# Another order of the front and some order ties in a three-layer kernel (attention, gated MLP, mixture of experts)

## The chip, the cores and the metric

The kernel runs on one core of a Trainium2 chip. The metric is the device time of one execution in microseconds. A core has a matrix engine (TensorE, PE in the profile), a vector engine (VectorE, DVE), an activation engine (ScalarE, ACT), a general engine (GpSimd, POOL), and a queue that issues the transfers (SyncE, SP). They run beside each other and wait for one another by semaphores; each works through its own instructions in the order in which the program put them.

## The reference, cut to what matters

Three layers follow one another. B=4 batches, 8 heads, S=576 positions, head size 64, 32 memory slots; 2304 tokens of width 512.

```python
a   = softmax(phi, over the sequence)            # 4 x 8 x 576 x 32 features, weights over slots
k_m = einsum('bhsm,bhsd->bhmd', a, k);  v_m = einsum('bhsm,bhsd->bhmd', a, v)
att = softmax(q @ k_m^T / 8);           x = att @ v_m         # -> 2304 x 512
x   = (sigmoid(x @ w_gate) * (x @ w_val)) @ w_out             # gated MLP, inner width 1536
p   = x @ w_gate2 + log1p(exp(x @ w_noise)) * noise           # router, top 2 of 8 experts
out = sum over the two experts: weight * relu(x @ w1[e]) @ w2[e]
```

## The kernel before

**What is computed where.** Nearly every product is made in fp16, with each fp32 operand split into a high and a low half, so that a product costs three matmuls. `memory` (L181) turns the features of one batch and one half of the heads (a "group", g=0 or 1): five transposes of phi against the identity `idf` (L189, L194), 40 small matmuls against the keys and values (L204), and a scaled copy `km` (L206). `attention` (L268) makes the scores of the queries (L284, L281) in three blocks: two large half blocks (u=0, 1: 512 columns) and a small one (u=2). For each block DVE takes the maximum `smx` (L288) and subtracts it (L292), ACT takes the exponential (L293). `normalised` (L296) sums and takes the reciprocal on DVE and multiplies on POOL (L304), and `turned` (L307) transposes the result on PE (L312) into the high and low halves of `x` (L321 on ACT, L322 on DVE).

**Stage 1** (L473) multiplies x with weights in which v_m is already contained: `fold(b, u)` (L245) scales v_m (POOL `vs`, L252), multiplies it with the weights of unit u (PE `pv`, L259, 32 records), and splits the product into `wq`: high half by ACT (L261), low half by DVE (L263; for the very first unit L1090). A unit and chunk of stage 1 are 24 matmuls (L485), a tanh on ACT (L487), a gate on DVE (L489), and a split into `gT` on ACT (L490) and DVE (L491). **Stage 2** multiplies gT with w_out (L502); `tokens` (L504) then takes the largest absolute value `am` of a tile on DVE (L514), scales it, and stores it for the experts.

**Weights.** w_gate, w_val and w_out come as halves of 512 KB. `rounded` (L368) turns one half in four steps: ACT L372, DVE L376 and L377, POOL L378. Two halves make one tile `w_n` (or `wo_n` for w_out), whose square sum (ACT L401, or L418 for w_out, into `wom`) goes through a matmul with ones (PE L93) and some short steps on DVE (L101 to L106) and POOL (L449, L450); only then is the scale known that `fold` needs. At the end the six w_out tiles are split by L434 (`split`: ACT, then DVE, 1024 columns). A buffer of a half is loaded again when it has been turned.

**What sets the order.** The program is written as generators. `turns` (in `build`) advances the attention generator and the weights generator; a list scheduler then orders each engine's instructions by priority, and `behind(d, o)` ties instruction d behind o on the same engine without a semaphore. At the start `turns(atts, atts, atts)` and FIRST=5 steps of `weights` come first; `half` then alternates a half of the weights with a step of the attention until the first x is there. `att_first_loads` (L168) gives the order of the first transfers on SP. Later `beside` runs the other batches, the folds, the tokens, and `presplits` (L680), which splits experts' weights ahead.

## Time and profile before

| | |
|---|---|
| runs of the kernel before | 852.46, 852.05, 851.23 us; median 852.05 us |
| profiled execution | 851.26 us, of which span 849.4 us, 1.86 us around it |
| mean granted TensorE clock | 0.991 |
| PE busy | 799.7 us of the span (94%) |
| DVE, ACT, POOL busy | 454.8, 440.0, 233.5 us |

Times in the profile count from the span's start. In the list by slices PE is 9 tenths busy or more from slice 5 on nearly everywhere; the first two slices (42 us) are the thin ones. So the table of all engines says that PE is the bound, and only the stretches where it waits can be shortened: the front up to the start of stage 1 (the first L485), and single waits after it.

### The profile page before, as it was taken

The numbers are of one execution on the slowest core, as the hardware profiler recorded it, in microseconds if no ns is written. First come the engines' busy times: TensorE is split into PE (matmuls) and PEld (weight loads), VectorE is DVE, ScalarE is ACT, GpSimd is POOL, SyncE is SP. The second block draws the span as 40 slices with busy tenths as digits, with TensorE's granted clock in tenths as the row PEclk, the third lists the DMA queues.
The fourth block names the chain that finished last, engine by engine and source line by source line (L and its number), as shares of the span: only waits on it lengthen the run. The fifth ranks groups of instructions, "written<-read, shape, count | busy, mean of one in ns | idle before, by whom it ended". The sixth has DMA issues, their size and how long they took to land.

```text
span 849.4 us, 16715 instructions
## 1 busy us (share of the span) xinstructions
PE 799.7 (94%) x6531; PEld 526.3 (62%) x6531; DVE 454.8 (54%) x1221; ACT 440.0 (52%) x859; POOL 233.5 (27%) x257
## 2 busy tenths in 40 slices
PE   5699889999999998999999999999999999999995
PEld 3478756476677665776556555746657475574752
DVE  3798996464558687645472365544445343450210
ACT  4687795155354665534263576645457364461320
POOL 1755650102203030231135342023133231232012
PEclk9999899999999999999999999999999999999998
DMA  9987669230312655617938899536767757463113
GB/s 315 349 263 242 231 202 319 78 106 2 76 58 98 181 172 151 215 47 184 280 103 217 167 240 208 176 75 129 190 150 126 207 117 171 74 124 39 23 23 40
DMA packets 124609, 130.95 MB, mean 154 GB/s; under 512 B 71664, under 2 KB 88176, under 8 KB 124144
## 3 DMA queue, kind: packets, MB, share of 16 engines
q1 hardware_dynamic: 114480, 109.10, 44.6%
q0 software_dynamic: 10048, 20.76, 13.5%
q8 instruction: 52, 0.85, 0.4%
q14 instruction: 29, 0.24, 0.1%
HBM read 85.87 MB, written 28.76 MB: 135 GB/s over the span
## 4 chain that ended last, share of the span: by engine, by line
PE 77%; DVE 9%; ACT 6%; DMA 3%; issue 2%; POOL 1%; SPq 0%; another core or an unknown queue 0%; DVEq 0%; ACTq 0%; POOLq 0%
PE ph L852 24%; PE py L866 23%; PE px L502 14%; PE pg L485 10%; PE pa L284 2%; PE pv L259 1%; DMA w<-wg 1%; DVE wq L263 1%; DVE pw L376 1%; DVE gT L491 1%; DVE pg L489 1%; PE pa L204 1%; ACT gT L490 1%; DMA wsp<-hl 1%; PE pl L530 1%
## 5 line engine op out<-in xcount | busy, mean ns | idle before, releaser
L485 PE MATMUL pg<-x,wq 128*128 128x192 f16 x1728 | 162.8, 249 | 11.7 <-DVE gT L491 4.2
L866 PEld LDWEIGHTS <-hT 128*128 128x128 f16 (+1 forms) x960 | 99.8, 105 | 104.8 <-DVE hT L858 1.2
L485 PEld LDWEIGHTS <-wq 128*128 128x128 f16 x1728 | 145.4, 99 | 31.2 <-issue 18.5
L502 PE MATMUL px<-wo,gT 128*128 128x512 f16 x648 | 147.7, 379 | 0.0
L874 POOL DMA_INDIRECT out<-y,mts x40 | 65.3, 1633 | 206.7 <-ACT y L873 204.3
L866 PE MATMUL py<-w2a,hT 128*128 128x512 f16 (+1 forms) x480 | 105.3, 379 | 0.7 <-DVE hT L858 0.7
L866 PE MATMUL py<-w2b,hT 128*128 128x512 f16 (+1 forms) x480 | 104.9, 379 | 0.0
L502 PEld LDWEIGHTS <-gT 128*128 128x128 f16 x648 | 61.7, 98 | 67.9 <-issue 2.3
L852 PE MATMUL ph<-xe,w1a 128*128 128x312 f16 (+2 forms) x768 | 103.3, 296 | 0.0
L852 PE MATMUL ph<-xe,w1b 128*128 128x312 f16 (+2 forms) x768 | 103.0, 296 | 0.0
L858 DVE TENSOR_TENSOR hT<-r,hT 128x312 f16<-128x312 f32 (+2 forms) x128 | 57.4, 480 | 84.7 <-ACT hT L857 78.6
L873 ACT ACTIVATE y<-py,css 128x512 f32<-128x512 f32 (+1 forms) x40 | 27.5, 687 | 124.5 <-PE py L866 115.5
L852 PEld LDWEIGHTS <-w1b 128*128 128x128 f16 x768 | 75.2, 98 | 27.1
L852 PEld LDWEIGHTS <-w1a 128*128 128x128 f16 x768 | 75.0, 98 | 27.1
L856 ACT ACTIVATE r<-ph 128x312 f32<-128x312 f32 (+2 forms) x128 | 49.7, 429 | 74.8 <-PE ph L852 68.6
L656 POOL DMA_INDIRECT meta<-mt,vi x36 | 38.5, 1069 | 121.3 <-DVE vi L653 81.1
L837 POOL DMA_INDIRECT xg<-xs,mts x40 | 45.2, 1130 | 81.5 <-DMA xe<-xg 47.7
L490 ACT ACTIVATE gT<-pg 128x384 f16<-128x384 f32 x72 | 35.1, 487 | 52.6 <-DVE pg L489 46.3
L487 ACT ACTIVATE sg<-pg,gss 128x384 f32<-128x384 f32 x72 | 41.9, 582 | 34.5 <-PE pg L485 33.6
L489 DVE SCALAR_TENSOR_TENSOR pg<-sg,pg 128x384 f32<-128x384 f32 x72 | 40.2, 558 | 35.0 <-PE pg L485 17.3
L857 ACT CAST hT<-r 128x312 f16<-128x312 f32 (+2 forms) x128 | 53.2, 458 | 0.9
L871 DVE TENSOR_TENSOR css<-mts,iw 128x1 f32<-128x1 f32 (+1 forms) x40 | 6.4, 163 | 87.3 <-ACT y L873 80.7
(241 smaller groups left out, 951.1 us busy)
## 6 DMA issues: line engine op xcount, KB each, us to landing
wo<-w SPq DMA_DIRECT2D x52, 512.0 KB
st<-kv SPq DMA_DIRECT2D x16, 512.0 KB
w<-wo SPq DMA_DIRECT2D x12, 512.0 KB
f<-w SPq DMA_DIRECT2D x12, 512.0 KB
wsp<-hl SPq DMA_DIRECT2D x12, 512.0 KB
out<-z SPq DMA_DIRECT2D x23, 256.0 KB
xs<-row SPq DMA_DIRECT2D x18, 256.0 KB
st<-q SPq DMA_DIRECT2D x6, 576.0 KB
```

The source lines that it names most:

```text
L485: self.gated = nc.tensor.matmul(p[:, f, :], w[:, l, g, j, f * P : (f + 1) * P], x[:, r, g, ch * QC : (ch + 1) * QC], start=n == 0, stop=n ...
L487: self.tanh = nc.scalar.activation(sg, ps[0], AF.Tanh, scale=self.gs[(b, u)])
L489: nc.vector.scalar_tensor_tensor(pv, sg, 1.0, pv, op0=ALU.add, op1=ALU.mult)
L490: self.gate = nc.scalar.activation(o[:, 0, :, cols], pv, AF.Copy, scale=2.0 ** -16)
L502: nc.tensor.matmul(p, g[:, l, f % 2, t * P : (t + 1) * P], self.wob[f // 2][:, r, f % 2, :], start=f + i == 0, stop=f == FT - 1 and i == 2)
L837: self.nc.gpsimd.indirect_dma_start(out=xg.rearrange("p a b -> p (a b)"), out_offset=None, in_=self.xs[:rows, :], in_offset=bass.IndirectO ...
L852: self.first = nc.tensor.matmul(p[:, : t1 - t0], w1[:, l, k, f * P : (f + 1) * P], xe[:, x, t0:t1], start=n == 0, stop=n == 3 * KT - 1)
L856: nc.scalar.activation(r, p[:, : t1 - t0], AF.Relu, scale=2.0 ** -19)
L857: d = nc.scalar.copy(self.hT[:, 0, f, t0:t1], r)
L858: self.parted = d, nc.vector.tensor_sub(self.hT[:, 1, f, t0:t1], r, self.hT[:, 0, f, t0:t1])
L866: d = nc.tensor.matmul(py, self.hT[:, l, f, i * P : i * P + m], w2[:, w, f, :], start=n == 0, stop=n == 3 * F2T - 1)
L874: d = nc.gpsimd.indirect_dma_start(out=self.out, out_offset=bass.IndirectOffsetOnAxis(ap=mt[:m, 0:1], axis=0), in_=y[:m], in_offset=None, ...
```

## The change

It does these things:

- The first transfers on SP come in another order: one half of the weights instead of two stands ahead of the keys of group 1, the queries of block 0 follow at once, and one half stands between them and those of block 1. FIRST is 2 instead of 5.
- The identity `idf` is made on DVE ahead of the maximum of phi; a one-column exponential `warm` at the start makes ACT load its function table there.
- For batch 0 the features of both groups are transposed first (one step of each `memory`), and only then come the matmuls with the keys. The first weights' conversion on ACT is tied behind the copies of those transposes (`laid`).
- Batch 0's attention normalises a half block one step behind its scores, as batch 1 does already, instead of all three blocks after the last scores.
- Ties: the first weights' square behind the first exponential (`exps`); w_out's squares behind the split of a gate (`gate`) instead of the tanh; `am` behind the last low half of a fold (`lows`); the squares and splits of the experts' weights behind the fold's casts or low halves too.

```diff
-FIRST = 5
+FIRST = 2
...
-        nc.vector.tensor_scalar(self.idf, jp, 0.0, None, op0=ALU.is_equal)
+        self.made = nc.vector.tensor_scalar(self.idf, jp, 0.0, None, op0=ALU.is_equal)
...
+        nc.scalar.activation(cp.tile([P, 1], F32, name="warm"), self.onef[:, :1], AF.Exp)
...
-        for x in (("phi", 0), ("phi", 1), ("kv0", 0), ("kv1", 0), "w", "w", ("kv0", 1), ("kv1", 1), "w", ("q", 0), "w", ("q", 1)):
+        for x in (("phi", 0), ("phi", 1), ("kv0", 0), ("kv1", 0), "w", ("kv0", 1), ("kv1", 1), ("q", 0), "w", ("q", 1)):
...
-        nc.scalar.copy(ag[:SH, SC, :], pt[:SH, 0, :])
+        self.laid = nc.scalar.copy(ag[:SH, SC, :], pt[:SH, 0, :])
...
-            nc.vector.tensor_reduce(mx, t, axis=AX.X, op=ALU.max, negate=True)
+            self.behind(nc.vector.tensor_reduce(mx, t, axis=AX.X, op=ALU.max, negate=True), self.made)
...
-                nc.vector.tensor_sub(t[:, 1, g], pv[g], t[:, 0, g])
+                self.lows = nc.vector.tensor_sub(t[:, 1, g], pv[g], t[:, 0, g])
...
-            nc.scalar.activation(ex, ex, AF.Exp, scale=0.125)
+            self.exps = nc.scalar.activation(ex, ex, AF.Exp, scale=0.125)
...
-            if b == 0 and i < 2:
-                yield
-                continue
-            for j in range(3) if b == 0 else (i - 1,) if b == 1 and i else (i,) if b > 1 else ():
+            for j in (i,) if b > 1 else (i - 1,) if i else ():
                 ex[j] = normalised(*part[j])
-                if b == 0:
-                    yield
-            if b:
-                yield
-        if b == 1:
+            yield
+        if b < 2:
             ex[2] = normalised(*part[2])
-        if b:
-            yield
+        yield
...
-        if self.tokens_ready:
-            self.behind(d, o or self.copied)
+        self.behind(d, (o or self.copied) if self.tokens_ready else self.laid)
...
-            if self.tokens_ready:
-                self.behind(d, self.copied)
+            if self.tokens_ready or not n:
+                self.behind(d, self.copied if n else self.exps)
...
-                if h == 0 and 2 <= n <= 12 and n % 2 == 0:
+                if h == (n == 4) and 2 <= n <= 12 and n % 2 == 0:
                     yield from finish(n // 2 - 1, WAIT_W)
...
-                    self.behind(nc.scalar.activation(junk, f, AF.Square, scale=self.iwv[x], accum_out=self.wom[:, x : x + 1]), self.tanh)
+                    self.behind(nc.scalar.activation(junk, f, AF.Square, scale=self.iwv[x], accum_out=self.wom[:, x : x + 1]), self.gate)
...
-        nc.vector.tensor_reduce(am, px, axis=AX.X, op=ALU.max, apply_absolute_value=True)
+        self.behind(nc.vector.tensor_reduce(am, px, axis=AX.X, op=ALU.max, apply_absolute_value=True), self.lows)
...
-            self.behind(d, self.less_gate if i % 2 else self.gate)
+            for o in ((self.gate, self.copied), (self.less_gate, self.lows))[i % 2]:
+                self.behind(d, o)
...
-                for d, o in zip(self.halved, (self.gate, self.less_gate)):
-                    self.behind(d, o)
+                for d, os in zip(self.halved, ((self.gate, self.copied), (self.less_gate, self.lows))):
+                    for o in os:
+                        self.behind(d, o)
...
-            yield from self.memory(b, 0)
-            yield from self.memory(b, 1)
+            ms = [self.memory(b, g) for g in range(2)]
+            if b == 0:
+                for m in ms:
+                    yield next(m)
+            for m in ms:
+                yield from m
...
-        turns(atts, atts, atts)
+        turns(atts, atts, atts, atts)
```

The order of the instructions moves by this at many places. Three of them follow.

SP, the first loads of the program (phi and st<-kv: features, keys and values; gT<-q: queries; w: halves of the weights). Before:

```order
L165 DMA phi<-phi 128x576 x2
L161 DMA st<-kv 128x4x256
L162 DMA st<-kv 64x256
L161 DMA st<-kv 128x4x256
L162 DMA st<-kv 64x256
L361 DMA w_153<-wg 128x2x512
L361 DMA w_155<-wg 128x2x512
L161 DMA st<-kv 128x4x256
L162 DMA st<-kv 64x256
L161 DMA st<-kv 128x4x256
L162 DMA st<-kv 64x256
L361 DMA w_163<-wv 128x2x512
```

After, from the same first weight on:

```order
L355 DMA w_155<-wg 128x2x512
L162 DMA st<-kv 128x4x256
L163 DMA st<-kv 64x256
L162 DMA st<-kv 128x4x256
L163 DMA st<-kv 64x256
L147 DMA gT<-q 128x576 x2
L355 DMA w_167<-wg 128x2x512
L147 DMA gT<-q 128x576 x2
L355 DMA w_173<-wv 128x2x512
L355 DMA w_175<-wv 128x2x512
```

One half of the weights has gone from ahead of group 1's keys, and two have gone from ahead of the last queries.

DVE, the end of the stretch in which the weights are prepared: the last splits of w_out (wo with wos), the low halves of a fold (wq), and the gates (pg<-sg,pg) and splits (gT) of stage 1. Before:

```order
L434 SCALAR_TENSOR_TENSOR wo_77<-wo_78,wos_1686,wo_77 128x1024
L491 SCALAR_TENSOR_TENSOR gT<-pg,gT 128x2x192
L263 TENSOR_TENSOR wq<-pv,wq 128x512 x2
L434 SCALAR_TENSOR_TENSOR wo_78<-wo_79,wos_1746,wo_78 128x1024
L489 SCALAR_TENSOR_TENSOR pg<-sg,pg 128x384
L434 SCALAR_TENSOR_TENSOR wr_1986<-wrf,wrs,wr_1985 128x64
L469 COPY itm_2950<-it_2948 64x1
L491 SCALAR_TENSOR_TENSOR gT<-pg,gT 128x2x192
L263 TENSOR_TENSOR wq<-pv,wq 128x512 x2
L489 SCALAR_TENSOR_TENSOR pg<-sg,pg 128x384
L491 SCALAR_TENSOR_TENSOR gT<-pg,gT 128x2x192
L489 SCALAR_TENSOR_TENSOR pg<-sg,pg 128x384
```

After:

```order
L264 TENSOR_TENSOR wq<-pv,wq 128x512 x2
L427 SCALAR_TENSOR_TENSOR wo_78<-wo_79,wos_1852,wo_78 128x1024
L482 SCALAR_TENSOR_TENSOR pg<-sg,pg 128x384
L101 TENSOR_SCALAR pmx<-pmx 128x1
L105 TENSOR_SCALAR wrs<-pmx 128x1
L106 TENSOR_SCALAR wri<-pmx 128x1
L427 SCALAR_TENSOR_TENSOR wo_79<-wo_80,wos_1912,wo_79 128x1024
L484 SCALAR_TENSOR_TENSOR gT<-pg,gT 128x2x192
L482 SCALAR_TENSOR_TENSOR pg<-sg,pg 128x384
L427 SCALAR_TENSOR_TENSOR wr_1988<-wrf,wrs,wr_1987 128x64
L427 SCALAR_TENSOR_TENSOR wo_80<-wo_81,wos_1916,wo_80 128x1024
L484 SCALAR_TENSOR_TENSOR gT<-pg,gT 128x2x192
```

Behind the last split of w_out there stood three gates, three splits of a gate and two low halves; now one split of a gate stands there, and the low halves and gates have gone ahead of the last splits.

DVE again, in the later stretch where stage 1 of the last batch runs beside stage 2: a square of the experts' weights (junk), the norm's sum (m), the fold's low halves (wq), and `am` of a tile with its short steps (tts, tti, itx). Before:

```order
L705 SCALAR_TENSOR_TENSOR junk,m<-f 128x1024
L514 TENSOR_REDUCE am<-px 128x1
L718 TENSOR_REDUCE m_4661<-m 128x1
L77 TENSOR_SCALAR tts<-am 128x1
L78 TENSOR_SCALAR tti<-tts 128x1
L79 TENSOR_SCALAR tts<-tti 128x1
L521 TENSOR_TENSOR itx<-tti,it_4516 128x1
L263 TENSOR_TENSOR wq<-pv,wq 128x512 x2
```

After:

```order
L698 SCALAR_TENSOR_TENSOR junk,m<-f 128x1024
L712 TENSOR_REDUCE m_4663<-m 128x1
L264 TENSOR_TENSOR wq<-pv,wq 128x512 x2
L507 TENSOR_REDUCE am<-px 128x1
L482 SCALAR_TENSOR_TENSOR pg<-sg,pg 128x384
```

The low halves have gone ahead of `am` and its short steps.

Elsewhere the squares of w_out on ACT come one tile later than before (the square of a tile stands behind the conversion of a half of the next), and at the first stage-1 matmul DVE has turned nine halves of the weights instead of twelve and a half.

## Rows read from the trace of the kernel before

**Rows 1.** The page, busy us, share of the span and instructions of each engine.

```profile
PE 799.7 (94%) x6531; PEld 526.3 (62%) x6531; DVE 454.8 (54%) x1221; ACT 440.0 (52%) x859; POOL 233.5 (27%) x257
```

**Rows 2.** Timeline of the front: start us, us, engine, line, operation [idle before <-releaser].

```profile
3.80 1.28 ACT L231 ACT_TABLE_LOAD   x1 [3.80 <-DMA phi<-phi]
5.09 0.77 ACT L231 ACTIVATE phi<-phi,pmx 128x576 f32<-128x576 f32 x1
...
7.02 0.21 DVE L116 TENSOR_SCALAR idf<-jp 128x128 f32<-128x128 f32 x1
...
7.37 1.09 PE L189 MATMUL pa<-idf,phi 128*128 128x128 f32 x4 [7.37 <-DVE new L945]
...
9.13 2.76 PE L204 MATMUL pa<-st,a 128*32 128x128 f32 x40 [0.46 <-ACT a L192]
...
10.90 0.71 ACT L372 ACTIVATE w<-w 128x512 int32<-128x512 uint32 x1 [1.66 <-DMA w<-wg]
...
16.05 1.47 PEld L204 LDWEIGHTS pa<-st,a 128*32 128x32 f32 x28 [0.20 <-DMA st<-kv]
...
18.70 0.47 ACT L206 ACTIVATE km<-pa,psm 128x256 f32<-128x256 f32 x1 [1.87 <-issue]
...
19.71 5.22 PE L284 MATMUL pa<-kbd,gT 128*128 128x64 f32 x24
...
23.26 0.69 DVE L288 TENSOR_REDUCE smx<-pa 128x16 f32<-128x512 f32 x1 [1.43 <-PE pa L284]
```

**Rows 3.** Timeline, from the first weights' norm to the first stage 1.

```profile
30.36 1.28 POOL L378 TENSOR_TENSOR w<-w,wo 128x512 int32<-128x512 int32 x1 [2.87 <-ACT ex L293]
...
31.68 1.06 ACT L401 ACTIVATE wo<-w 128x1024 bf16<-128x1024 f32 x1 [1.10 <-POOL w L378]
...
32.33 0.62 POOL L252 TENSOR_TENSOR vs<-vb,wss 128x256 f32<-128x256 f32 x1
...
33.00 2.42 PE L259 MATMUL pv<-w,vs 64*32 64x256 f32 x32 [4.21 <-POOL vs L252]
...
35.00 0.59 ACT L261 CAST wq<-pv 128x512 f16<-128x512 f32 x1 [1.60 <-PE pv L259]
```

**Rows 4.** Timeline of PE and DVE at the start of stage 1.

```profile
43.39 4.94 PE L485 MATMUL pg<-x,wq 128*128 128x192 f16 x44 [0.40 <-DVE wq L1090]
...
44.05 0.68 DVE L1090 TENSOR_TENSOR wq<-pv,wq 128x512 f16<-128x512 f32 x1
```

**Rows 5.** One stretch: its us, each engine's busy us and count, clock, DMA.

```profile
44.00:134.00 90.00, 80.41 (x1043) 63.79 (x1041) 82.53 (x182) 72.76 (x148) 47.56 (x72) 0.96 0.76 247
```

**Rows 6.** Timeline of ACT and PE at the longest PE wait of that stretch, and neighbours.

```profile
77.08 1.92 PE L284 MATMUL pa<-kbd,st 128*128 128x64 f32 x16
...
94.18 1.15 ACT L418 ACTIVATE wo<-wo,swi 128x1024 bf16<-128x1024 f32 x1 [0.92 <-POOL wo L378]
...
97.13 2.08 PE L485 MATMUL pg<-x,wq 128*128 128x192 f16 x12 [2.56 <-DVE gT L491]
...
112.46 1.15 PE L485 MATMUL pg<-x,wq 128*128 128x192 f16 x12 [1.36 <-ACT sg L487]
```

**Rows 7.** PE alone by stretch: us, busy us (count), granted clock, DMA share, GB/s.

```profile
98.00:100.00 2.00, 1.33 (x10) 0.50 1.01 290
```

**Rows 8.** Timeline of DVE at the end of the weights' preparation.

```profile
114.58 0.16 DVE L423 TENSOR_REDUCE wom<-wom 128x1 f32<-128x6 f32 x1 [1.55 <-ACT wo L418]
...
141.31 0.56 DVE L489 SCALAR_TENSOR_TENSOR pg<-sg,pg 128x384 f32<-128x384 f32 x1 [2.57 <-PE pg L485]
```

**Rows 9.** Timeline of PE and DVE beside the last batch's folds.

```profile
326.53 1.24 PE L259 MATMUL pv<-w,vs 64*32 64x256 f32 x32 [2.27 <-DVE wq L263]
...
329.62 0.69 DVE L514 TENSOR_REDUCE am<-px 128x1 f32<-128x512 f32 x1
...
330.85 1.28 DVE L263 TENSOR_TENSOR wq<-pv,wq 128x512 f16<-128x512 f32 x2
...
331.59 2.14 PE L485 MATMUL pg<-x,wq 128*128 128x192 f16 x24 [1.45 <-DVE wq L263]
```

## The prediction

> **What bounds the kernel now.** I read the busy times first: PE works 94% of the span [rows 1], so a change can win only where PE waits or runs at half its pace. Then I read the timeline of the front, where PE has least to do, and looked at each step for the wait that ended last [rows 2 to 4]. Stage 1 is in full flow only once the second low half of the first fold is there, at 44.05 + 0.68 = 44.7 us [rows 4]. Third comes the stretch from there to the end of the weights' preparation, as one sum [rows 5]: of 90 us PE is busy 80.4 and DVE 82.5. Both are nearly full, so work pushed from the front into this stretch isn't free: DVE has 7.5 us left there, PE 9.6. Last I looked for single waits of PE: 2.56 us at 97 us [rows 6], and 2.27 and 1.45 us near 330 us [rows 9]. Behind 150 us PE is nearly gapless, so what is won or lost before reaches the end.
>
> **The front, step by step.** The table load takes 1.28 us between phi's arrival and the first exponential [rows 2]; with `warm` it is done while phi is still on its way. The maximum of phi starts with phi's arrival and takes 0.74 us (half of 1.48 for two), so the exponential starts at about 4.55 instead of 5.09. The identity now waits for nothing on DVE's queue; before, it stood behind both exponentials and ended at 7.23, with the transposes at 7.37 [rows 2]. So they can start at about 5.5, 1.9 us earlier. I cost that at no gain by itself: the 40 matmuls of group 0 need its keys, and the loads that are ahead of them are the same in both kernels. They began at 9.13 [rows 2], and the first half of the weights, which is next in the queue, had landed by 10.90; nothing lets the keys come before about 9.2. They end at about 11.9 in both.
>
> Group 1 does gain. Between the first weights (10.90) and the last keys (16.05) [rows 2] there landed one 0.52 MB half and two 0.59 MB blocks of keys, 1.70 MB in 5.15 us, 0.33 MB/us. So a half of the weights taken from ahead of the keys moves them by 0.52 / 0.33 = 1.6 us, to 14.2 to 14.5. Group 1's transposes and copies are done by then, and PE waits for the keys alone. The scaled copy `km` of group 1, at 18.70 before, follows at about 16.9. The queries come ahead of three halves now, so the scores start at about 17.9 (19.71), and the first maximum is at 21.45 instead of 23.26 [rows 2]. **1.8 us** is gained up to there; between 1.3 (a slower load) and 1.9 (all of what the transposes gain).
>
> From the first maximum to stage 1 there are two chains. By DVE alone it would be shorter: before, this was 44.7 - 23.3 = 21.4 us, filled with work; of the halves, 3.5 fewer are turned before stage 1, 2 of them from the stretch ahead of the first maximum and 1.5 from this one. 1.5 halves at 1.27 us (two steps of 0.68, overlapping a little) give 1.9 us, so by DVE the gain could be 3.7. The other chain is the first fold's: its second tile needs the fourth half, whose place in the queue is now behind all queries; by the bytes ahead of it, it lands at 21.9. DVE reaches its second step behind the second exponential's operands, at about 30. POOL adds in 1.28, to 31.25, ACT squares in 1.06 [rows 3], to 32.5. The norm's matmul and the short steps on DVE and POOL take about 2.8, and `vs` ends at 35.95 where it ended at 32.95 before [rows 3]. The 32 records of `pv` take 2.42 [rows 3], and eight transposes of the exponentials now stand between them, at 1.09 per four [rows 2]: 40.6. Two casts at 0.59 [rows 3] with a copy of x between them and the low half at 0.68 end at about 43.1. So stage 1 flows **1.6 us** earlier (44.7 before); the range is 0 to 3.7, and I take the value of the fold's chain, since it is the longer one.
>
> **What is pushed behind.** 3.5 halves x 1.27 = **4.4 us** of DVE work now stand behind the start of stage 1. ACT (0.66 each) and POOL (1.28) have more room there [rows 5], DVE has not. Against that, two things shorten DVE's way to the end of the preparation. First, the sum of w_out's squares waited 1.55 us for ACT with DVE idle [rows 8]; now casts, gates and low halves stand about it. I take 0.9 of it, between 0 and 1.55. Second, behind the last split of w_out three gates and three splits of gates (0.56 each [rows 8]) and two low halves (1.28 for two [rows 9]) still followed, 6 x 0.56 + 1.28 = 4.6 us; now one of 0.56 follows. That work is ahead of the splits, where PE's last matmuls of the stretch can use it: **4.1 us** less behind them, between 2 (if PE's last units, which waited for PE itself at 141.31 [rows 8], are bound by PE) and 4.1. Sum of the stretch: -1.6 + 4.4 - 0.9 - 4.1 = **-2.2 us**, and with the ends of each, +2.4 to -4.9.
>
> **The ties.** Near 330 us PE waits 1.45 us for a fold's low halves [rows 9], which stand behind `am` and its short steps on DVE. Between the start of `am` at 329.62 and the low halves at 330.85 are 1.23 us, of which the sum m (0.15) stays: **-1.1 us**, since what stands behind the low halves then, the token's scaling, has no one waiting near. The wait of 2.27 just before [rows 9] hangs on a transfer that frees a buffer on ACT; ACT's order there is the same, and I leave it. The tie of w_out's squares may shorten the 2.56 us wait [rows 6]; I count nothing, and it is a rival. The ties of the experts' squares and splits change places of instructions with no PE wait behind them; 0, between -1 and +1. Queues passed: SP issues the same transfers; of those that follow, one half of the weights goes ahead of another by the time a buffer is free, no more.
>
> **The sum.** -2.2 - 1.1 = **-3.3 us**. The profiled execution was 851.26 (span 849.4 and 1.86 around it), so 848.0; the median of the runs, 852.05, lies 0.8 above it, so I expect **848.7** as median.
>
> **A rule weighed.** After the 2.56 us wait, 12 matmuls took 2.08 us that take 1.15 elsewhere [rows 6], and the granted clock reads 0.50, which is the 1.2 GHz level [rows 7]. The Trainium skill, page "TensorE: Matmul & The Clock Gate", section "What's actually happening", says that the default state is throttled and that activity releases the throttle. By that rule a front with its PE work closer together could have its clock released earlier, and the scores' 24 matmuls would cost half. The trace speaks against it: those 24 take 5.22 us inside a stretch that PE fills without a gap [rows 2], 0.22 each, and the same form took 0.12 later [rows 6]. As a mechanism here: if the scores ran at 0.12, the first maximum would come another 1.4 us earlier (14 of the first 16 records at 0.10 less); the fold's chain, which waits for its weights, would keep stage 1 where it is, and the time would be 848.7 still to 848.0. I give it 3 in 100, within the first case.
>
> **The rivals.** *Given back:* DVE is the bound of the stretch, so the pushed halves eat what the front and the tail win, and only the tie of -1.1 stays: 852.05 - 1.1 = **850.9**. For it speaks that DVE is 92% busy [rows 5]; against it that the last matmuls wait for PE, not DVE [rows 8]. The same time comes if the change doesn't do what it says, a front whose stage 1 starts no earlier with as much hidden as now. *Slower:* the fold's chain gets later, since the fourth half now lands behind the queries, stage 1 starts no earlier than 44.7, and the 4.4 us show, less the 1.55 of idle DVE time and the tie: +4.4 - 1.55 - 1.1 = +1.75, **853.8**; with stage 1 1.5 us late 855.3. It decides where the second low half ends: from 44.7 on this case holds. For it speaks that `vs` by my own count is 3 us later than before; against it that stage 1 waited for x and DVE's queue, not for `vs`. *More won:* the squares of w_out, one tile later, no longer hold ACT for POOL (0.92 at 94.18), so the wait of 2.56 us and the half pace behind it vanish. The half pace cost 0.93 per 12 matmuls, with 34 such records and 4 transposes about 2.9 us: up to 5.5 together, of which DVE's fullness lets half through: 852.05 - 3.3 - 2.75 = **846.0**. Against it: the same stretch has 4.4 us more DVE work, and a new wait as long would keep the clock where it is.
>
> **How the numbers follow.** Forecast 50%, its own range 847.0 to 850.3 (stage 1 earlier by 0 to 3.7 with the tail between its ends); given back 22%; slower 15%; more won 13%. A measurement of this kernel can tell 0.2%, 1.7 us, from no change: faster is below 850.3, slower above 853.8. The forecast but for 3 parts and the last case are faster: 0.60; given back and those 3: 0.25; slower: 0.15. The range is 845.5 to 854.0: it leaves out the far half of the slow case, and the deeper ends of the last one.
>
> **What would show it.** Right: the first maximum at 21 to 22 us, the second low half by 43.5, the last gate that waits for PE (141.31 before) by 139.5, and no PE wait over 0.5 at 330. Wrong: if the first maximum comes early but stage 1 does not, the fold's chain was under-counted; if PE waits for DVE more often between 44 and 134, the pushed halves were not hidden; if the clock column dips at another place than 96 to 104, a new wait has come.

## The result, and the profile after

The changed kernel takes 860.88 us (median of 7 runs, 859.82 to 867.58), the kernel before 851.93 us beside it (7 runs). The ratio is **1.0121, 95% interval 1.0094 to 1.0148**: about 10 us slower, where 848.7 us was forecast, in a range that ended at 854.0.

The first profile of the changed kernel fell on its longest execution, 867.58 us. The rows below are from a second profile of the same kernel (the run `again`), an execution of 859.88 us with span 858.1, unless the text says otherwise. Its busy times, to be set against [rows 1]:

```profile
PE 800.8 (93%) x6531; PEld 525.4 (61%) x6531; DVE 453.9 (53%) x1221; ACT 441.9 (52%) x860; POOL 233.5 (27%) x257
```

The work is the same. Of the 8.7 us more of span 7.6 are idle time of PE (57.3 us instead of 49.7) and 1.1 its busy time. The timeline of the front says that the loss is not there:

```profile
0.73 1.28 ACT L120 ACT_TABLE_LOAD   x1 [0.73 <-PEq L1241]
...
4.43 0.78 ACT L232 ACTIVATE phi<-phi,pmx 128x576 f32<-128x576 f32 x1 [2.20 <-DVE pmx L230]
...
5.35 1.12 PE L190 MATMUL pa<-idf,phi 128*128 128x128 f32 x4 [5.35 <-ACT phi L232]
...
14.21 2.50 PE L205 MATMUL pa<-st,a 128*32 128x128 f32 x36 [0.18 <-DMA st<-kv]
...
16.86 0.47 ACT L207 ACTIVATE km<-pa,psm 128x256 f32<-128x256 f32 x1 [2.60 <-issue]
...
21.32 0.69 DVE L289 TENSOR_REDUCE smx<-pa 128x16 f32<-128x512 f32 x1 [2.65 <-PE pa L285]
...
34.87 0.62 POOL L253 TENSOR_TENSOR vs<-vb,wss 128x256 f32<-128x256 f32 x1
...
41.17 1.28 DVE L1089 TENSOR_TENSOR wq<-pv,wq 128x512 f16<-128x512 f32 x2
```

The reader is to compare with [rows 2 to 4]: the last keys land at 14.2 instead of 16.05, the first maximum starts at 21.3 instead of 23.26, and the second low half ends at 42.45 instead of 44.7. Stage 1 flows 2.3 us earlier. (In the first profile it ends at 42.97.) The loss lies behind that. One stretch, 43 to 100 us, of the kernel before and then of the changed one (us; busy us of PE, weight loads, DVE, ACT, POOL with counts; granted clock; DMA share; GB/s):

```profile
43.00:100.00 57.00, 50.38 (x654) 42.33 (x655) 51.39 (x114) 44.54 (x97) 33.61 (x41) 0.97 0.77 246
```

```profile
43.00:100.00 57.00, 46.11 (x596) 38.78 (x596) 46.48 (x106) 39.47 (x86) 27.30 (x33) 0.91 0.65 210
```

Every engine does less in the same time, DVE too (82% of the stretch instead of 90%), and the transfers move less: no engine is full there. What PE waits for, 43 to 150 us (total us, times, longest), in the changed kernel, its three longest sums:

```profile
PE pv L260 <- POOL vs L253: 8.7, 3, 5.2
PE pg L478 <- DVE gT L484: 4.8, 4, 2.7
PE pmx L93 <- ACT wo L394: 3.0, 4, 0.9
```

The kernel before has no wait of PE for `vs` in this stretch; its longest sum is this, and all its waits there come to 10.5 us, against 19.9 in the changed kernel:

```profile
PE pg L485 <- DVE gT L491: 3.5, 3, 2.6
```

The longest wait for `vs`, in the timeline:

```profile
82.81 1.93 PE L285 MATMUL pa<-kbd,st 128*128 128x64 f32 x16
...
83.25 0.16 DVE L101 TENSOR_SCALAR pmx<-pmx 128x2 int32<-128x2 int32 x1
...
84.78 0.69 DVE L289 TENSOR_REDUCE smx<-pa 128x16 f32<-128x512 f32 x1 [0.79 <-PE pa L285]
...
87.28 0.10 DVE L105 TENSOR_SCALAR sws<-pmx 128x2 int32<-128x2 int32 x1
...
89.38 0.27 POOL L442 TENSOR_SCALAR wss<-sws,sv0s 128x2 f32<-128x2 f32 x1
...
89.97 0.62 POOL L253 TENSOR_TENSOR vs<-vb,wss 128x256 f32<-128x256 f32 x1
...
90.64 2.06 PE L260 MATMUL pv<-w,vs 64*32 64x256 f32 x32 [5.24 <-POOL vs L253]
```

The norm of the fifth unit's weights is known at 83.4 (L101), but its last steps stand on DVE behind the scores of batch 1 and come at 87.28. POOL first multiplies a block of batch 1 (87.50 to 88.55) and sets batch 1's scales, and makes vs at 89.97. PE, which has no other unit left, stands still for 5.24 us. So this wait itself comes from where the norm's steps stand; the unit's four halves were turned by then. And the last half of the weights is ready on POOL 15 us later than before (19.6 in the first profile). First the kernel before, 110.75 + 2.53 = 113.3, then the changed one, 127.06 + 1.29 = 128.4:

```profile
110.75 2.53 POOL L378 TENSOR_TENSOR wo<-wo,w 128x512 int32<-128x512 int32 x2
```

```profile
127.06 1.29 POOL L371 TENSOR_TENSOR wo<-wo,w 128x512 int32<-128x512 int32 x1 [0.25 <-ACT w L366]
```

The gapless stage 2 begins at 147.53 in the kernel before and at 156.23 in the changed one, 8.7 us later; that is the whole difference of the spans (in the first profile 160.83, 13.3 us later):

```profile
147.53 12.68 PE L502 MATMUL px<-wo,gT 128*128 128x512 f16 x58
```

```profile
156.23 10.09 PE L495 MATMUL px<-wo,gT 128*128 128x512 f16 x46
```

### The profile page after: what moved, and what is told of

It reads as the page before. It is cut to its first block, busy times and chain, and to the rows that moved or that the text cites. A ratio compares the mean times of both kernels' runs of the same rounds, so it can differ in the third digit from the quotient of the medians.

```text
span 865.8 us, 16723 instructions
## 1 busy us (share of the span) xinstructions
PE 807.2 (93%) x6531; PEld 528.6 (61%) x6531; DVE 453.2 (52%) x1221; ACT 442.3 (51%) x860; POOL 230.6 (27%) x257
## 3 DMA queue, kind: packets, MB, share of 16 engines
q0 software_dynamic: 10048, 20.76, 13.4%
## 4 chain that ended last, share of the span: by engine, by line
PE 77%; DMA 6%; DVE 6%; ACT 5%; issue 2%; POOL 1%; SPq 1%; another core or an unknown queue 0%; DVEq 0%; POOLq 0%; ACTq 0%
PE py L861 23%; PE ph L847 21%; PE px L495 14%; PE pg L478 11%; PE pv L260 2%; DMA w<-wo 2%; PE pa L285 2%; DMA wo<-w 1%; PE pa L205 1%; DMA st<-kv 1%; DMA xg<-xs,mts 1%; ACT wo L394 1%; PE pl L523 1%; DVE wq L264 1%; PE pmx L93 1%
## 5 line engine op out<-in xcount | busy, mean ns | idle before, releaser
L478 PEld LDWEIGHTS <-wq 128*128 128x128 f16 x1728 | 147.5, 100 | 26.8 <-issue 12.5
L861 PE MATMUL py<-w2b,hT 128*128 128x512 f16 (+1 forms) x480 | 106.7, 383 | 2.3 <-DVE hT L853 2.3
L482 DVE SCALAR_TENSOR_TENSOR pg<-sg,pg 128x384 f32<-128x384 f32 x72 | 40.2, 558 | 36.2 <-PE pg L478 19.6
L260 PE MATMUL pv<-w,vs 64*32 64x256 f32 x768 | 37.1, 422 | 18.0 <-POOL vs L253 11.6
```

The source lines that it names most:

```text
L260: self.combined = nc.tensor.matmul(pv[g][32 * h : 32 * h + 32, j, :], vs[rows, j, h, :], self.W[2 * u + j][rows, h, :], start=True, stop=T ...
L478: self.gated = nc.tensor.matmul(p[:, f, :], w[:, l, g, j, f * P : (f + 1) * P], x[:, r, g, ch * QC : (ch + 1) * QC], start=n == 0, stop=n ...
L482: nc.vector.scalar_tensor_tensor(pv, sg, 1.0, pv, op0=ALU.add, op1=ALU.mult)
L861: d = nc.tensor.matmul(py, self.hT[:, l, f, i * P : i * P + m], w2[:, w, f, :], start=n == 0, stop=n == 3 * F2T - 1)
```

## The experiments

**The theory**, called head start: what counts is how many halves of the weights are turned when stage 1 begins. A unit of stage 1 needs its fold, the fold needs vs, that needs the norm, and that needs all four halves of the unit; the halves in turn are tied on ACT behind the folds' casts and stand on DVE between gates. With a lead of about a unit (three gates) nobody waits; with less, folds wait for weights and weights for folds. **The rivals**: the ties; the new order of batch 0's scores; the new order of the loads; the half pace of PE behind each wait.

The lead can be read from the order of DVE's instructions. One letter a step: h a half turned, G a gate of stage 1, [ and ] begin and end of a norm's short steps, q a low half of a fold, S a maximum of scores, x a low half of x, v the norm of batch 1's values (that of batch 0's is left out); a space stands ahead of a gate:

```
before    hhhhShS[h]hShh[]hxhxqhxqh Gh G[h]qq Gh Gh Ghq[q] Ghhh Gh G[hv]qq
after     hhShShhS[]hhxhxhxqq[h G] Ghqqh Gh G[] Ghhhqqh G Gh[h] Ghhqqh GS Gv[hS] Ghhqq
a_first5  hhhhShS[]hhShhx[hx]qhxqh Gh G[h]qq Gh Ghh G[]qqh Ghh Gh G[hv]qq
a_head3   hhShShhS[]hhxhxhxh[h]qhqhh G G[q]q Ghh Ghh G[h]qqh Ghh Gh G[]vhqq
a_att     hhShShhS[]hhhxhxqhxq[]h G Ghhqq G G[h] Ghhqhq Gh G[h]h Ghqqh GS Gv[h] GhSqq
```

Before the first G there are 13 h in the kernel before and 10 in the changed one, and the second norm, over before the first gate there, straddles it here. Each kernel below was timed against the kernel before on the same chip; "last half" is the end of the last L378 (L371) on POOL in its profile, 113.3 in the kernel before. That column is one execution each: the first profile of the changed kernel has 132.9 where the second has 128.4, so differences of under 5 us in it are not to be read.

| run | halves ahead of the first gate | last half, us | ratio to before, 95% interval |
|---|---|---|---|
| again (the changed kernel) | 10 | 128.4 | 1.0137 (1.0081 to 1.0193) |
| a_noties | 10 | 128.3 | 1.0129 (1.0072 to 1.0186) |
| a_fill | 10 | 126.4 | 1.0111 (1.0080 to 1.0142) |
| b_first | 11 | 121.9 | 1.0079 (1.0039 to 1.0120) |
| a_att | 11 | 118.3 | 1.0021 (0.9994 to 1.0049) |
| b_att | 12 | 116.9 | 1.0082 (1.0057 to 1.0108) |
| a_weights | 12 | 117.4 | 1.0034 (1.0018 to 1.0051) |
| a_first5 | 12 | 116.8 | 1.0029 (1.0007 to 1.0051) |
| b_loads | 13 | 112.9 | 0.9984 (0.9963 to 1.0005) |
| b_first2 | 13 | 117.7 | 1.0034 (1.0010 to 1.0058) |
| b_att1 | 13 | 113.0 | 0.9974 (0.9956 to 0.9993) |
| b_mid | 13 | 111.1 | 0.9975 (0.9962 to 0.9989) |
| b_head1 | 14 | 115.0 | 1.0009 (0.9993 to 1.0024) |
| a_head3 | 14 | 114.8 | 1.0026 (1.0009 to 1.0043) |

**The changed kernel again, with FIRST=5, and without the ties.**

> The changed kernel once more, for a second profile, since the first one was taken of an execution (867.58 us) 6.7 us above its own median of 860.88. Both theories: 860 to 862 us. If PE's long waits for the scaled values vs (2.4 us at 76, 5.2 us at 94) and the half pace behind them are the loss, then a profile of an execution near the median shows the same waits, with fewer or shorter stretches at a granted clock of 0.50.

```diff
-FIRST = 2
+FIRST = 5
...
-            if self.tokens_ready or not n:
-                self.behind(d, self.copied if n else self.exps)
+            if self.tokens_ready:
+                self.behind(d, self.copied)
```

> The changed kernel with FIRST=5 again (and the first square not tied behind the exponential, which that needs): DVE then has 12 halves of the weights instead of 10 ahead of the first gate (13 before). Theory head start (too few halves are ready when stage 1 begins, so that folds wait for weights, and weights for folds): the loss goes, 849 to 853 us, and the last half is ready near 113 us as before. Rival, the ties of w_out's squares and of the later order: stays at 859 or more.

```diff
-... accum_out=self.wom[:, x : x + 1]), self.gate)
+... accum_out=self.wom[:, x : x + 1]), self.tanh)
...
-        self.behind(nc.vector.tensor_reduce(am, px, axis=AX.X, op=ALU.max, apply_absolute_value=True), self.lows)
+        nc.vector.tensor_reduce(am, px, axis=AX.X, op=ALU.max, apply_absolute_value=True)
```

(and the experts' squares and splits as before)

> The changed kernel with its later ties undone (w_out's squares behind the tanh again; the largest absolute value and the experts' squares and splits as before). The front is the changed one. Theory head start: 860 to 863 us, up to 1.1 slower than the changed kernel, since the low halves near 330 us stand behind the largest absolute value again. Rival (ties): 850 to 853 us.

FIRST=5 takes most of the loss away (854.97 us, where 849 to 853 was expected; the kernel before was at 853.19 beside it). Undoing the later ties takes nothing away (1.0129 against 1.0137); they are not the cause. FIRST=2 alone in the kernel before:

```diff
-FIRST = 5
+FIRST = 2
```

> The kernel before with FIRST=2 alone: 11 halves instead of 13 ahead of the first gate on DVE. Theory head start: slower, 856 to 861 us, with PE waits for vs of over 2 us between 60 and 100 us. Rival (ties or the new order of the scores): within 1.5 us of the kernel before.

It costs 1.0079, as expected, although the waits have another name there: PE waits for gT (6.0 us at stage 1 and 3.3 at the folds), not for vs; that part of the expectation missed.

**The order of the scores, and the halves given back elsewhere.** First the changed kernel with the old order of batch 0's scores:

```diff
-            for j in (i,) if b > 1 else (i - 1,) if i else ():
+            if b == 0 and i < 2:
+                yield
+                continue
+            for j in range(3) if b == 0 else (i - 1,) if b == 1 and i else (i,) if b > 1 else ():
                 ex[j] = normalised(*part[j])
+                if b == 0:
+                    yield
...
```

> The changed kernel with the old order of batch 0's scores (all three blocks first, then their normalisation), FIRST=2 and the new loads kept; 11 halves ahead of the first gate on DVE. Theory head start: stays slow, 1.009 to 1.016 of before, since the folds still run short of weights. Rival (the new order of the scores is the loss): 1.000 to 1.004.

This missed. It has 11 halves, waits for vs five times (7.2 us in all), and is still only 1.0021. So the number of halves is not all. The norms' steps lie better in it (the second norm is over before the first gate, and no score stands inside the fifth one), and its last half is ready at 118.3; whether that is the reason is not shown. To see whether the order costs by itself, it was put alone into the kernel before, then with one half given back:

```diff
-            if b == 0 and i < 2:
-                yield
-                continue
-            for j in range(3) if b == 0 else (i - 1,) if b == 1 and i else (i,) if b > 1 else ():
+            for j in (i,) if b > 1 else (i - 1,) if i else ():
                 ex[j] = normalised(*part[j])
...
+            yield
...
+        for _ in range(1):
+            half()
         t, pv = self.low
```

> The kernel before with the new order of batch 0's scores alone. It has one step of the attention less before stage 1, so 12 halves instead of 13 stand ahead of the first gate. Theory head start: 1.002 to 1.006 of before. Rival (the order of the scores is neutral or good by itself, as the prediction took it): 0.996 to 1.000.

> The kernel before with the new order of batch 0's scores and one more half turned ahead of the first stage 1, so 13 halves again. Theory head start (the order costs only by the half that it takes away): 0.999 to 1.002 of before. Rival (the order itself costs): 1.005 or more, as without the half (1.0082).

The order alone costs 0.8%, more than expected; with the one half that it had taken away it costs nothing (0.9974). This is the clearest pair: the two kernels differ by one half of the weights ahead of stage 1, and their intervals lie far apart. The same for the changed kernel, with three halves given back and all else kept, and for FIRST=2 alone:

```diff
+        for _ in range(3):
+            half()
         t, pv = self.low
```

> The changed kernel with three more halves of the weights turned between the last score and the first stage 1, nothing else: 13 halves ahead of the first gate on DVE, as in the kernel before, but with FIRST=2, the new loads and the new order of the scores kept. Theory head start: most of the loss goes, 0.997 to 1.003 of before, although stage 1 starts up to 4 us later than in the changed kernel. Rival (the score order or the loads cost by themselves, wherever the halves stand): 1.008 or more.

> The kernel before with FIRST=2, and two more halves turned between the last score and the first stage 1: 13 halves again. Theory head start: 0.999 to 1.003 of before, against 1.0079 with FIRST=2 alone. Rival (the place of the halves counts, not their number): 1.006 or more.

Both come back to 1.003. In a_head3 the order of DVE has 14 halves ahead of the first gate, not the 13 that were expected: the gate comes later too, at 49.76 us (45.03 in the changed kernel). In a_head3 the front, FIRST=2, the loads and the score order are the changed kernel's, and PE waits no more for vs. Its three longest sums of waits, and stage 2:

```profile
PE pg L478 <- DVE gT L484: 5.5, 6, 1.5
PE pg L478 <- ACT sg L480: 2.8, 2, 2.1
PE pg L478 <- DVE wq L1091: 2.2, 1, 2.2
```

```profile
150.92 15.27 PE L495 MATMUL px<-wo,gT 128*128 128x512 f16 x70
```

**Loads and norms.** The changed kernel with FIRST=5, the old loads and the old place of the norms; then the new loads alone in the kernel before:

```diff
-... ("kv1", 0), "w", "w", ("kv0", 1), ("kv1", 1), "w", ("q", 0), "w", ("q", 1)):
+... ("kv1", 0), "w", ("kv0", 1), ("kv1", 1), ("q", 0), "w", ("q", 1)):
```

(for a_weights the other way round, with FIRST = 5, the first square untied, and `if h == 0 and 2 <= n <= 12` again)

> The changed kernel with FIRST=5 and also the old order of the first loads (two halves ahead of group 1's keys) and the old place of the norms; the scores' new order and the ties stay. Theory head start: like FIRST=5 alone or better, 0.998 to 1.003 of before. Rival (the half blocks' new order costs by itself): 1.005 or more.

> The kernel before with the new order of the first loads alone; 12 halves ahead of the first gate, as the order of DVE has it. The keys of group 1 land 1.6 us earlier. Theory head start: a half lost against a start up to 1.5 us earlier, 0.999 to 1.004 of before. The prediction's front (the earlier keys are what wins): 0.997 to 0.999.

The old loads add nothing to FIRST=5 (a_weights can't be told from a_first5), and the new ones cost nothing alone. The expectation of b_loads counted one half too few: in its trace 13 halves stand ahead of the first gate, as before. The keys land at 15.03 instead of 16.05, and the second low half ends at 44.3 instead of 44.7. So this run doesn't weigh a lost half against earlier keys.

**The clock.** Around the wait of 5.24 us the granted clock falls: 1.00 from 78 to 85.4 us, with PE busy throughout, and 0.50, the 1.2 GHz level, from 90.6 to 92.6, behind the wait. 16 useless matmuls ahead of the two folds that waited longest keep PE busy:

```diff
+        if b == 0 and u in (3, 4):
+            for _ in range(16):
+                nc.tensor.matmul(pv[0][:, 0, :P], self.idf, self.onef, start=True, stop=True)
```

> The changed kernel with 16 matmuls without a use in front of the fold of units 3 and 4 of batch 0, where PE waits for vs (2.4 and 5.2 us); their result is overwritten. They keep PE busy for about 2.4 us there. If the half pace behind the waits is a main part of the loss: granted clock 1.00 behind those folds and 2 to 5 us faster than the changed kernel. If the waits themselves are the loss: no faster than the changed kernel, at 1.012 or more.

One stretch, 43 to 150 us, of the changed kernel and of this one:

```profile
43.00:150.00 107.00, 87.88 (x1133) 69.16 (x1133) 89.03 (x197) 80.33 (x163) 49.84 (x77) 0.90 0.68 220
```

```profile
43.00:150.00 107.00, 92.88 (x1244) 74.84 (x1248) 91.14 (x199) 82.24 (x169) 49.80 (x77) 0.98 0.72 226
```

The clock is 0.98 there instead of 0.90, and the waits for vs are down to 1.0 us (the order moved too: the fifth norm is no longer parted by scores), while the folds' waits for low halves rose from 2.2 to 4.4 us. The time is still 1.0111, at least 0.8% above the kernel before by its interval, and the last half comes at 126.4. So the half pace and that one wait are not the main part of the loss. A small part, some 1 to 2 us of the 10, they may be: 1.0111 can't be told from 1.0121 or 1.0137, and the useless matmuls may cost something themselves. The late weights fit what is left.

**What else was tried for a gain.** The later ties alone, the same with the front's parts that take no half away, one more half than before, and the parts that won together. For b_mid, put into the kernel before:

```diff
+                self.lows = nc.vector.tensor_sub(t[:, 1, g], pv[g], t[:, 0, g])
...
+        self.behind(nc.vector.tensor_reduce(am, px, axis=AX.X, op=ALU.max, apply_absolute_value=True), self.lows)
...
+            for o in ((self.gate, self.copied), (self.less_gate, self.lows))[i % 2]:
+                self.behind(d, o)
```

(and the same for the splits); b_frontmid adds to it `idf`, `warm`, `laid` and the two `memory` steps of the change, b_head1 one `half()` as above, best0 the score order and one `half()`, best1 the loads too.

> The kernel before with the ties of the later part alone (the largest absolute value behind the fold's low halves, the experts' squares and splits behind casts and low halves). The prediction's term: 1.1 us faster, 0.9985 to 0.9990 of before, and no PE wait over 0.5 us at the low halves near 330 us. Rival (nothing waits less in sum, the wait only moves): 0.9997 to 1.0005.

> The kernel before with the later ties, and of the front only what takes no half of the weights away: identity and table load early, both groups' features transposed first; loads, FIRST and the order of the scores as before, so 13 halves ahead of the first gate. Theory head start: not slower than before, 0.997 to 0.9995. Rival (the transposes ahead of the first weights' conversion delay the first halves as much): 1.000 or more.

> The kernel before with the later ties and one more half of the weights ahead of stage 1 (14 instead of 13). Theory head start, if 13 is still short: 0.994 to 0.9965 of before. If 13 is enough: 0.9975 to 0.999, a later start that the slack doesn't pay for.

> The kernel before with the new order of batch 0's scores, one more half of the weights ahead of stage 1, and the later ties: the two parts that won by themselves (0.9974 and 0.9975). If they add: 0.994 to 0.996 of before. If the ties' gain is one that the other part has already taken: 0.997 to 0.998.

> The same with the new order of the first loads too (0.9984 by itself). Theory head start: with 13 halves still ahead of the first gate the earlier keys add a little, 0.992 to 0.996 of before. Rival (the halves that now stand last before stage 1 make the start as late as the keys made it early): no better than without them.

b_frontmid gave 0.9994 (0.9979 to 1.0010), best0 0.9995 (0.9977 to 1.0012), best1 1.0005 (0.9985 to 1.0024). b_mid and b_att1 are each 0.25% faster than before by their own intervals, yet together they are not. The order of b_mid on PE, DVE and ACT is that of the kernel before up to about 200 us, and yet its profile has stage 2 at 145.4 instead of 147.5. So differences of a quarter per cent between two programs are not to be read as gains of a part here, and no version that clearly beats the kernel before was found. Fourteen halves are no better than thirteen.

## Why the prediction was wrong, step by step

- **The front: right.** Predicted: first maximum 21.45, vs 35.95, second low half 43.1, start 1.6 us earlier. Measured: 21.3, 35.5 and 42.45 (21.8, 36.0 and 42.97 in the first profile), 1.7 to 2.3 us earlier. The matmuls of group 0 were costed to end at 11.9 in both; they ended at 10.52 instead of 11.89, but what they feed waited for the keys of group 1 until 14.2, so that brought nothing, as costed.
- **What is pushed behind: the step that failed.** The 3.5 halves were priced as 4.4 us of DVE time, to be hidden in DVE's idle time and paid back by the tail. In the traces they are 3: ahead of the second low half DVE has turned 12 halves before and 9 after (the front's twelve and a half is too many), 3.8 us at the same price. But DVE was not what bounds: its busy time from 43 to 100 fell from 51.4 to 46.5 us. The halves are the first link of a chain (four halves, square, norm, vs, pv, cast), and turning fewer ahead shortens the lead of that chain over PE. The mistake was to count the work of the halves and not who waits for them, and when. The stretch was to give -2.2 us; it gave +8.7 (156.23 against 147.53). The sign of being wrong looked at DVE as well: PE's waits for DVE from 44 to 134 us were 5 instead of 7 (6.2 us in all instead of 4.5), and what is new are 8.7 us of waits for POOL's `vs`. The other sign came true, the clock dips at new places (0.57 from 73 to 77 us, 0.50 from 90.6 to 92.6).
- **The way the loss grows** was seen nowhere: a fold that is late delays the casts behind which the next halves are tied, and so the lead isn't regained. The last half was 15 us late, from 3 halves fewer, which are 3.8 us of DVE work. That the ties behind the casts do this is read from the code and the trace; no run took them away.
- **The tail** (4.1 us) was read from a mark of the loss. Behind the last split of w_out little follows in the changed kernel because that split itself comes late. The last split in the kernel before, in the changed one, and in a_head3:

```profile
132.88 1.28 DVE L434 SCALAR_TENSOR_TENSOR wo<-wo,wos,wo 128x1024 f16<-128x1024 f32 x1
```

```profile
150.02 1.28 DVE L427 SCALAR_TENSOR_TENSOR wo<-wo,wos,wo 128x1024 f16<-128x1024 f32 x1
```

```profile
134.27 1.28 DVE L427 SCALAR_TENSOR_TENSOR wo<-wo,wos,wo 128x1024 f16<-128x1024 f32 x1 [0.56 <-ACT wo L426]
```

  It is 17.1 us late in the changed kernel, and stage 2 only 8.7. In a_head3, with the same ties and the weights nearly in time, three gates, four splits of gates and four low halves stand behind it again, and stage 2 begins 15.4 us behind its end (13.4 in the kernel before). The idle 1.55 us of DVE are gone as expected, but the sum of w_out's squares that ends them comes at 129.75 instead of 114.58, so nothing is won by it.
- **The tie of the low halves: right in place.** 1.1 us was expected from the wait of 1.45 us [rows 9]. The low halves now go first and PE waits 0.40:

```profile
339.43 1.28 DVE L264 TENSOR_TENSOR wq<-pv,wq 128x512 f16<-128x512 f32 x2
340.16 2.14 PE L478 MATMUL pg<-x,wq 128*128 128x192 f16 x24 [0.40 <-DVE wq L264]
340.62 0.68 DVE L507 TENSOR_REDUCE am<-px 128x1 f32<-128x512 f32 x1
```

  That is 1.05 us. Whether it shows in the time stays open: alone it was 0.9975, with other parts nothing.
- **The rival that ended slower** named the right things (the fold's chain, the pushed halves) but priced them at 1.75 to 3.3 us, and took as its point of decision a second low half at 44.7 or later. That half ended at 42.5 and the kernel was still 10 us slower: the first fold was in time, the later ones were not. A count of gates on DVE points there: between a unit's norm and its fold's low halves stand two or three gates in the kernel before and one in the changed one, from the second unit on.
- **The rule weighed.** The front stayed at half pace: 22 scores took 4.79 us in both profiles, 0.22 each, as before, against 0.12 at 82.81. The granted clock of 18 to 24 us doesn't settle it: it reads 0.50 in the second profile and 1.00 in the first and in the kernel before, at the same pace. Behind the wait of 5.24 us it reads 0.50, ahead of it 1.00. The Trainium skill says on its page "TensorE: Matmul & The Clock Gate", section "What's actually happening", that the default state is throttled and that activity releases the throttle. The trace around that wait agrees: behind it the clock reads 1.00 again from 95 us, when PE has worked on. a_fill shows that this was little of the loss.
- **The sums** hold, but for the forecast's own range: a start 3.7 us earlier gives 846.6, not 847.0, and a tail of 2 gives 850.8, above 850.3.

**What stays open.** That halves turned ahead of stage 1 are the loss is shown by giving them back: b_att and b_att1, and the changed kernel and a_head3, each with intervals far apart; b_first and b_first2 go the same way, with intervals that overlap. The single parts (FIRST=2 1.0079, score order 1.0082, loads 0.9984, ties 0.9975) come to 1.012 together, which is what the whole cost. By the same sum a_first5 and a_att would each be at 1.004; they measured 1.0029 and 1.0021, with 1.004 inside their intervals. So the parts add up as far as these runs tell. What one half costs doesn't come out of them: FIRST=2 takes two halves away and costs 0.8%, the score order takes one and costs as much. b_att and a_weights both have 12 halves, the same order of letters up to 102 us and their last half at 116.9 and 117.4, yet 1.0082 and 1.0034, with intervals that don't meet. a_att, with 11 halves and from the third unit on one gate between norm and fold as in the changed kernel, is nearly free of the loss. How the loss follows from the number of halves, the gates between norm and fold, and the place of the norms' steps is argued from the order and the trace, not shown.

## What to carry to other kernels

A preparation that runs ahead of its consumer is worth its lead, not its busy time: before taking work from ahead of a loop, count at each turn of the loop how far the producer's chain, down to its last short step, is ahead, and be wary where that lead goes under one turn. An earlier start of the consumer cuts the lead a second time. A busy share near full on one engine doesn't say that it is the bound: here DVE's fell from 90% to 82% while the kernel got slower. And an order read from the changed program, like the short tail here, can be the mark of a delay and not its cure: ask why it moved.

## What was not expected of the hardware

Two executions of the same program, with the same order of instructions, were 7.7 us apart (spans 865.8 and 858.1). From 44 to 46 us the granted clock was 0.50 in the longer one and 1.00 in the other, with half as many matmuls done (PE alone: us, busy us and count, clock, DMA share, GB/s; first the longer one):

```profile
44.00:46.00 2.00, 2.00 (x14) 0.50 0.99 368
```

```profile
44.00:46.00 2.00, 2.00 (x28) 1.00 0.97 366
```

Just before, PE had done the same in both: it waited 0.94 us for a square and then began these 40 matmuls, first in the longer execution, then in the other:

```profile
44.03 4.86 PE L478 MATMUL pg<-x,wq 128*128 128x192 f16 x40
```

```profile
43.03 3.46 PE L478 MATMUL pg<-x,wq 128*128 128x192 f16 x40
```

Why the clock fell in one and not in the other is not shown. The kernel before spreads as widely on another chip (847.87 to 858.31 us in 16 runs), so one profile of either can fall far from its median.
